# An unused 128 KB read of w_in put first on ScalarE's queue, in a kernel of chunked retention and a feed-forward block

## The chip, the core and the metric

The kernel runs on one core of a Trainium2 chip. The time is device microseconds (us) of one execution. The kernel before was timed in three runs: median 210.21 us, from 209.93 to 211.16 us. A profile was taken of one further execution.

The engines are named as in the profile: PE is TensorE (with PEld for its weight loads), DVE is VectorE, ACT is ScalarE, POOL is GpSimd and SP is SyncE. A transfer (DMA) is issued by one engine into that engine's queue, and its packets are then moved by the core's 16 DMA engines, which all queues share.

## The reference, cut to what matters

Two steps follow each other. The first is a recurrent retention layer: batch 4, 8 heads, 768 positions, head dimension 64, with one decay rate per head. The second is a feed-forward layer on the 3072 resulting rows, with a "snake" activation between its two matrix products.

```
gamma = 1.0 - 2.0 ** (-5.0 - np.arange(H))
for t in range(S):
    state = gamma * state + einsum('bhd,bhe->bhde', k[:, :, t], v[:, :, t])
    y[:, :, t] = scale * einsum('bhd,bhde->bhe', q[:, :, t], state)
x = y.transpose(0, 2, 1, 3).reshape(B * S, H * D)      # 3072 x 512
h = x @ w_in                                           # 3072 x 2048
s = np.sin(alpha * h)
g = h + s * s / (alpha + 1e-09)
out = g @ w_out                                        # 3072 x 512
```

Inputs and output are float32. The kernel computes its products in bf16.

## The kernel before, in words

**Tiling.** The recurrence is done in 24 chunks of 128 positions (6 per batch). A chunk is worked out with matrix products: scores inside the chunk, a decay mask, and for the later chunks of a batch a product with a running 64x64 state per head. The finished chunks, transposed, are collected in groups xT of 4, 2, 2, ..., 2, 4 chunks (`sizes`), and each group goes through the feed-forward: `Slot` does 128 columns of `x @ w_in` for a group (L496), the sine and the square on ACT (L499, L504) or DVE (L506), and the sum on DVE (L511); `ff_out` multiplies by w_out (L521); `take` and `last_tile` copy the sums out of PSUM and store them. The four first chunks of the batches, e0 to e3, need no state and come first.

**What sets the order.** The order of every engine's instructions is written out by hand, in program order (the pool's automatic scheduling is switched off by `manual_schedule`), and each engine works its list off in order. What ties the engines together is semaphores: an instruction waits for the data that it reads, and a transfer for the semaphore "lane" that an earlier transfer used (8 lanes for POOL's transfers, 8 for those of SP and ACT together, each used in turn).

**The start.** This is the part around the change.

- SP issues three transfers: q of chunk e0, then k of chunk e0 (L141, float32, 1024 pieces of 256 bytes each, tiles named `o_sb` because they borrow the buffers of the output), and alpha (L144).
- POOL issues all other loads, and they turn float32 into bf16 on the way: v of e0, then q, k, v of e1 and e2 (L100), the first quarter of w_in in two halves (L131), q and k of e3, the first quarter of w_out in two halves (L135), v of e3, the second quarters, and so on. Between them it computes small tables (L165 `tok`, L229 `qg`). From its ninth transfer on, one of POOL's transfers also waits until the one eight places earlier has landed.
- ACT loads the table for the exponential (L178), fills the decay table `dec` with eight activations (L190), turns k of e0 into bf16 (L576), and then copies results and fills `qg` (L569) until the first sine.
- DVE builds constants, turns q of e0 into bf16 (L574), and applies masks to scores (L286).
- PE fills its time with `idle_work`: matmuls on a zero tile, `spare<-warm` (L566), 25 in all, in counts written between the real steps. The first 9 stand ahead of the first real work, the transposes of q of e0 (L250). The real steps then are transposes (L250), scores (`stage_A`, L282), mixing with v (`stage_M`, L312), and from the group of e0 to e2 on the feed-forward.

ACT issues one transfer of its own in the kernel before, a 64 KB piece of the output at the very end (L553). Lines are those of the kernel before; behind the change the numbers are higher by 2.

Of the kernel before, what the change touches and what calls it, by code (L numbers as in the profile page):

```python
# [8 lines left out]
F32 = mybir.dt.float32  # L9
# [7 lines left out]
def kernel(  # L17
# [15 lines left out]
    nc = tc.nc  # L33
# [22 lines left out]
    consts = ctx.enter_context(tc.tile_pool(name="consts", bufs=1))  # L56
# [9 lines left out]
    w_in_v = moe_w_in.rearrange("(ko ki) f -> ki ko f", ki=128)  # L66
# [105 lines left out]
    load_w_out(1)  # L172


    warm = consts.tile([128, 512], BF16, name="warm")
    nc.vector.memset(warm, 0.0)  # L176
    tiny = consts.tile([128, 1], F32, name="tiny")
# [642 lines left out]
```

## Time and profile before

| what | value |
|---|---|
| time, median of 3 runs | 210.21 us (209.93 to 211.16) |
| the profiled execution's own time | 210.45 us |
| its span (first to last instruction) | 208.7 us |
| PE busy | 202.4 us, 97% of the span |
| DVE, ACT, POOL busy | 152.7, 151.6, 116.2 us |
| queue of POOL's transfers (software_dynamic) | 79248 packets, 13.38 MB |
| queue of SP's transfers (hardware_dynamic, q1) | 22608 packets, 10.96 MB |
| queue of ACT's one transfer (hardware_dynamic, q10) | 144 packets, 0.07 MB |
| read from and written to HBM | 27.27 MB and 6.29 MB |

How to read it: the span is what the profile covers, and the profiled execution's own time is 1.75 us longer. PE runs its list in order, so the end is the sum of its busy time and of the gaps in it; a gap counts when PE waits for something. The row DMA in the page's 40 slices shows how busy the 16 DMA engines were, in tenths. The list of transfers gives the time from issue to landing, which contains the wait behind earlier transfers.

### The profile page before, as it was taken

The page shows a single profiled execution, that of the slowest core. Times are in us where ns is not written, and L with a number is a line of the kernel's source. Part 1 is how long each engine was busy: PE and PEld are TensorE (multiplying, and loading weights), DVE is VectorE, ACT ScalarE, POOL GpSimd, SP SyncE. Part 2 cuts the span into 40 slices and gives each one's busy share as a digit, 9 for nine tenths or more (in the row PEclk, how much of TensorE's full clock was granted, in tenths as well). Part 3 has the DMA queues.
Part 4 walks back from the last instruction along what each step waited for, and adds up shares of the span by engine and source line. Part 5 has one row for each costly group of instructions (what it writes and reads, how often), then busy time and mean ns, then how long its engine had stood idle before and what let it go on. Part 6 is the DMA issues. An engine that isn't in the chain of part 4 may idle for free.

```text
span 208.7 us, 5765 instructions
## 1 busy us (share of the span) xinstructions
PE 202.4 (97%) x2370; PEld 123.7 (59%) x2370; DVE 152.7 (73%) x314; ACT 151.6 (73%) x309; POOL 116.2 (56%) x157
## 2 busy tenths in 40 slices
PE   7988999999999999999999999999999999999994
PEld 2444544467776766766666766666766664444453
DVE  5788688877989968768878868868888965656220
ACT  7777777657998787787687787686785779999001
POOL 8999847599999999999699910002022200000000
PEclk9999999999999999999999999999999999999999
DMA  9999999999999999999999996422412101010212
GB/s 132 148 167 194 202 201 185 154 168 196 162 115 154 104 187 171 170 110 194 171 117 169 152 143 53 104 60 44 105 56 48 53 2 50 2 50 3 101 50 101
DMA packets 102026, 24.76 MB, mean 119 GB/s; under 512 B 93024, under 2 KB 99056, under 8 KB 102000
## 3 DMA queue, kind: packets, MB, share of 16 engines
q0 software_dynamic: 79248, 13.38, 86.9%
q1 hardware_dynamic: 22608, 10.96, 24.0%
q8 instruction: 18, 0.29, 0.6%
q10 hardware_dynamic: 144, 0.07, 0.1%
q14 instruction: 8, 0.07, 0.1%
HBM read 27.27 MB, written 6.29 MB: 161 GB/s over the span
## 4 chain that ended last, share of the span: by engine, by line
PE 79%; DMA 9%; POOL 9%; issue 1%; DVE 0%; POOLq 0%; DVEq 0%
PE po L521 35%; PE ph L496 33%; DMA w_out<-in_moe_w_out_dram 5%; DMA qkr<-in_k_dram 5%; POOL qkr L100 3%; PE py L336 2%; POOL qg L229 2%; POOL vr L100 2%; PE poh L546 2%; POOL w_in L131 2%; PE py L390 1%; POOL w_out L135 1%; PE pa L346 1%; PE py L399 1%; PE pt L264 1%; PE pa L353 1%
## 5 line engine op out<-in xcount | busy, mean ns | idle before, releaser
L511 DVE SCALAR_TENSOR_TENSOR gT<-s,rec_alpha,ph 128x256 bf16<-128x256 f32 (+3 forms) x164 | 79.9, 523 | 31.7 <-ACT s L504 31.3
L496 PE MATMUL ph<-xT,w_in 128*128 128x256 bf16 (+3 forms) x656 | 98.6, 291 | 0.3 <-ACT xT L314 0.2
L499 ACT ACTIVATE s<-ph,alpha_sb 128x256 f32<-128x256 f32 (+3 forms) x164 | 76.1, 506 | 30.3 <-PE ph L496 30.2
L521 PE MATMUL po<-w_out,gT 128*128 128x512 bf16 x368 | 95.4, 380 | 0.0
L496 PEld LDWEIGHTS <-w_in 128*128 128x128 bf16 x656 | 63.3, 98 | 33.9 <-issue 1.2
L504 ACT ACTIVATE s<-s 128x512 f32<-128x512 f32 (+1 forms) x91 | 56.9, 625 | 2.9
L521 PEld LDWEIGHTS <-gT 128*128 128x128 bf16 x368 | 33.9, 98 | 29.6 <-DMA w_out<-in_moe_w_out_dram 0.2
L467 POOL CAST s_q<-s_f 128x256 bf16<-128x256 f32 x5 | 2.0, 396 | 35.6 <-DVE s_f L452 19.2
L533 DVE COPY o_sb<-po 128x512 f32<-128x512 f32 x20 | 13.8, 690 | 9.9 <-PE po L521 9.8
L120 POOL DMA_DIRECT2D qk_seq<-in_q_dram x24 | 16.9, 780 | 2.1 <-DMA v_seq<-in_v_dram 2.0
L120 POOL DMA_DIRECT2D qk_seq<-in_k_dram x24 | 16.9, 739 | 0.6 <-DMA qk_seq<-in_q_dram 0.5
L120 POOL DMA_DIRECT2D v_seq<-in_v_dram x24 | 16.9, 772 | 0.0
L156 POOL TENSOR_TENSOR v_seq<-v_seq,kgq 128x512 bf16<-128x512 bf16 x13 | 13.7, 1078 | 4.9 <-DMA v_seq<-in_v_dram 4.9
L441 DVE TENSOR_TENSOR xT<-py,qg 128x512 bf16<-128x512 f32 x19 | 13.0, 683 | 0.8 <-PE py L406 0.8
L361 DVE TENSOR_TENSOR aTw<-pa,maskq 128x768 bf16<-128x768 f32 x13 | 12.4, 951 | 0.0
L100 POOL DMA_DIRECT2D vr<-in_v_dram x11 | 10.2, 929 | 1.2 <-DMA w_in<-in_moe_w_in_dram 1.1
L566 PE MATMUL spare<-warm 128*128 128x512 bf16 x25 | 8.7, 471 | 1.2 <-DVE warm L176 1.2
L550 ACT COPY o_sb<-poh 128x256 f32<-128x256 f32 (+1 forms) x2 | 0.6, 319 | 11.7 <-PE poh L546 11.2
L349 DVE TENSOR_TENSOR aT<-pa,mask 128x1024 bf16<-128x1024 f32 x7 | 8.5, 1216 | 0.0
L467 ACT CAST s_q<-s_f 128x256 bf16<-128x256 f32 x14 | 5.5, 391 | 3.1 <-DVE s_f L461 2.7
L100 POOL DMA_DIRECT2D qkr<-in_k_dram x7 | 6.3, 899 | 1.7 <-DMA w_out<-in_moe_w_out_dram 1.7
L100 POOL DMA_DIRECT2D qkr<-in_q_dram x7 | 6.4, 910 | 1.0 <-DMA w_in<-in_moe_w_in_dram 1.0
(101 smaller groups left out, 162.3 us busy)
## 6 DMA issues: line engine op xcount, KB each, us to landing
out_dram<-o_sb SPq DMA_DIRECT2D x23, 256.0 KB, 3.0
w_in<-in_moe_w_in_dram POOLq DMA_DIRECT2D x6, 256.0 KB, 10.8
w_out<-in_moe_w_out_dram POOLq DMA_DIRECT2D x3, 512.0 KB, 11.0
vr<-in_v_dram POOLq DMA_DIRECT2D x11, 128.0 KB, 5.1
qk_seq<-in_q_dram POOLq DMA_DIRECT2D x16, 80.0 KB, 6.3
qk_seq<-in_k_dram POOLq DMA_DIRECT2D x16, 80.0 KB, 4.9
v_seq<-in_v_dram POOLq DMA_DIRECT2D x16, 80.0 KB, 5.6
qkr<-in_q_dram POOLq DMA_DIRECT2D x7, 128.0 KB, 5.7
```

Source lines behind the costliest of these rows:

```text
L100: nc.gpsimd.dma_start(out=t, in_=chunk_of(src, j))
L120: nc.gpsimd.dma_start(out=o, in_=src[bt, head(b, m, e), cs[0] * C:, :].rearrange("(f i) d -> i f d", i=64))
L156: eng.tensor_mul(t, t, by[:, j % NCH, :, None].to_broadcast([128, H, D]))
L361: return {"mask": lambda: nc.vector.tensor_mul(aT, pa[:, :, 0:384].rearrange("p e (m t) -> p e m t", m=2), maskq[:, None, None, :].to_broa ...
L441: nc.vector.tensor_mul(o, st["pyw", old][:, :, 0:256].rearrange("p b (m t) -> p b m t", m=2), by)
L496: nc.tensor.matmul(self.ph[:, m, :], w_in[:, i, f * 128:(f + 1) * 128], xT[g][:, i, self.lo:self.hi], start=(m == 0 and i == 0), stop=(i = ...
L499: nc.scalar.activation(out=self.s[:, m, :], in_=self.ph[:, m, :], func=ACTF.Sin, scale=alpha_sb[:, f:f + 1])
L504: nc.scalar.activation(out=self.s, in_=self.s, func=ACTF.Square)
L511: nc.vector.scalar_tensor_tensor(gT[self.g][:, f, self.lo:self.hi], self.s[:, m, :], rec_alpha[:, f:f + 1], self.ph[:, m, :], op0=ALU.mult ...
L521: nc.tensor.matmul(po[g, ts], gT[g][:, f, ts * C:(ts + 1) * C], w_out[:, f, :], start=(f == 0), stop=(f == FF - 1))
L533: nc.vector.tensor_copy(o_sb, po[g, ts])
L566: nc.tensor.matmul(spare["ps"], warm[:, :128], warm, start=True, stop=True)
```

## The change

Two lines are put ahead of ACT's first instruction. A new tile of 128 partitions by 256 float32 (1 KB in each partition) is allocated in the pool of constants, and ACT issues a transfer into it from the first 128 rows and first 256 columns of w_in, in float32, without a cast. Nothing reads the tile. The same numbers are still loaded by POOL as before.

```diff
     load_w_in(1)
     load_w_out(1)
 
+    wake = consts.tile([128, 256], F32, name="wake")
+    nc.scalar.dma_start(out=wake, in_=w_in_v[:, 0, 0:256])
     warm = consts.tile([128, 512], BF16, name="warm")
     nc.vector.memset(warm, 0.0)
     tiny = consts.tile([128, 1], F32, name="tiny")
```

The order of instructions on every engine is otherwise the same: ACT has one more, the transfer, ahead of its first table load, and PE, DVE, POOL and SP have the same lists. Since the lanes of SP's and ACT's transfers are used in turn, each later one of these has the next lane (q of e0 now signals on the second lane instead of the first, and so on), with the same distance of eight. The tiles allocated after `wake` lie 1 KB further on in each partition.

## The prediction

> **What bounds the kernel now.** I read the page first, for the engines and the chain.
>
> ```profile
> PE 202.4 (97%) x2370; PEld 123.7 (59%) x2370; DVE 152.7 (73%) x314; ACT 151.6 (73%) x309; POOL 116.2 (56%) x157
> ...
> PE   7988999999999999999999999999999999999994
> ...
> DMA  9999999999999999999999996422412101010212
> ...
> q0 software_dynamic: 79248, 13.38, 86.9%
> ```
>
> PE is busy for 202.4 of 208.7 us, with a fixed list of instructions, so all gaps of PE together are 6.3 us. The DMA row is full from the first slice to the twenty-fourth (about 125 us): a transfer added in that time can only displace others. Next, the timeline of the first 21 us (start, duration, engine, line, what, count, idle before), for the place of the change.
>
> ```profile
> 0.74 1.28 ACT L178 ACT_TABLE_LOAD   x1 [0.74 <-PEq L804]
> 0.74 0.46 SPq L141 DMA_DIRECT2D o_sb<-in_q_dram  x1
> ...
> 1.19 4.02 PE L566 MATMUL spare<-warm 128*128 128x512 bf16 x9 [1.19 <-DVE warm L176]
> ...
> 2.52 2.45 ACT L190 ACTIVATE dec<-tio,back 128x128 f32<-128x128 f32 x8 [0.28 <-DVE mask L192]
> ...
> 3.92 0.55 DVE L574 CAST qb<-o_sb 128x512 bf16<-128x512 f32 x1 [0.42 <-DMA o_sb<-in_q_dram]
> ...
> 4.58 0.15 PEld L250 LDWEIGHTS <-qb 128*128 128x128 bf16 x1 [0.28 <-DVE qb L574]
> 5.00 0.61 PE L250 MATMUL pt<-ident,qb 128*128 128x128 bf16 x4
> ...
> 5.17 0.62 ACT L576 CAST kb<-o_sb 128x512 bf16<-128x512 f32 x1 [0.21 <-DMA o_sb<-in_k_dram]
> ...
> 20.42 0.41 PE L312 MATMUL pye<-aT,vr 128*64 128x128 bf16 x8 [0.66 <-DMA vr<-in_v_dram]
> ```
>
> PE has fillers until about 5.0 us, while q of e0 is ready at 4.47 (3.92 + 0.55): q has some 0.42 us in hand (weights at 4.58, matmul at 5.00). k of e0 has none: ACT stands idle 0.21 us for it. Later, at 20.42, PE stands 0.66 us for v of e3, whatever happened before. Last, the chain in order of time up to 41 us (start, duration, what).
>
> ```profile
> 16.76 3.98 POOL qg L229 x4
> 20.74 9.94 DMA w_out<-in_moe_w_out_dram
> 30.68 0.28 issue
> 30.96 9.53 DMA qkr<-in_k_dram
> ...
> 40.54 0.41 PE pt L264 x8
> ```
>
> The chain runs through POOL's transfers until 40.54 us and through PE alone after that. So what a few hundred ns in the start are worth is decided by one question: do POOL's transfers land later? PE has idle time of 0.26 us between 40 and 60 us and almost none from 60 to 160, so a shift at 40.54 reaches the end whole.
>
> **The change, part by part.**
>
> *Nothing is removed.* No wait on the data of the new tile exists. The lanes of SP's and ACT's later transfers move by one with the same distance of eight, and the unused read has landed tens of us before its lane comes up again. I cost that at nothing.
>
> *ACT's instruction.* One issue ahead of the table load. Rows: SP's first issue takes 0.46 us, ACT's own issue at the end 0.37, SP's second 0.56. ACT starts at 0.74, so the table load ends 0.37 to 0.56 later, at 2.39 to 2.58 instead of 2.02, and `tiny` (0.20) at 2.59 to 2.78. `dec` started at 2.52 after 0.28 idle on DVE's mask, so it moves by 0.07 to 0.26 and ends at 5.04 to 5.23. The next on ACT is k at 5.17, which waits for its transfer anyway: ACT costs at most 0.06 us, taken as 0. The cover is the idle 0.28 and 0.21; without it all 0.37 to 0.56 would go to k. DVE reads `dec` first at 5.99, so it does not notice.
>
> *The packets, on SP's two loads.* 128 packets of 1 KB, 131 KB. The nearest row is the first half quarter of w_in on POOL's queue, which reads the same kind of 1 KB pieces (and writes 512 bytes): from 11 to 13 us 708 packets went through in 2 us, 354 per us. 128 of them take 0.36 us of all 16 engines. The other bound is SP's rate for 256 byte pieces, about 280 GB/s around 3 us: 131 KB / 280 = 0.47 us. From below, the read can fall into time when the DMA engines have nothing to do: the first packets of q start 1.1 us after their issue and ACT's last transfer starts its packets 0.88 us after its own, so the read can be up to 0.26 us ahead of q; then 0.1 us is left, and if it is quicker still, 0. I take 0.36, since the two issues start at the same 0.74 us and both find an idle chip. q then is ready at 4.83, inside its 0.42 of cover: nothing. k lands at 5.53 instead of 5.17 and PE's transposes of it, with all that follows on PE, ACT and DVE, move by 0.36. This lasts until 20.42, where the 0.66 us of waiting for v of e3 swallows it. What counts from there is how late v of e3 comes.
>
> A rule of the Trainium skill, "DMA: Bandwidth & Descriptors", section "Issuing engines are not separate DMA queues", says that transfers issued by different engines run on the same 16 DMA engines and interleave; by it the read delays q, k and POOL's loads alike. By the ceiling of 435 GB/s of the same page ("Where 436 GB/s comes from") the 131 KB would take an estimated 0.30 us, which is 0.06 us less than the row's 0.36 and would lower the sum below by as much.
>
> *The packets, on POOL's loads.* The engines are busy from about 2 us on, so 0.36 us of work is pushed ahead of POOL's first load. Can they catch up? From 5 to 9.5 us POOL's queue moved 5296 packets, 1177 per us, and every load landed 4.5 to 4.7 us after its issue: no backlog builds up, POOL's issuing (0.87 us for 1024 packets, 1177 per us) sets the pace. From 37.5 to 41 us, behind a backlog, the same kind of packet went at 4291 in 3.5 us, 1226 per us. So the DMA engines have 49 of 1226, 4%, to spare, over some 5 us (4.6 to 9.6): 0.20 us is caught up. After that w_in comes in, the time to landing grows (7.6 us for v of e3, issued at 12.81) and nothing more can be caught up until 40 us. So v of e3 and all later loads come 0.36 - 0.20 = 0.16 us later. Bounds: 0 (the read fits in idle time or is caught up) and 0.47 (none caught up). POOL's issues wait for landed transfers and move by the same 0.16.
>
> *Sum.* PE at 20.42 moves by 0.16, at 40.54 by 0.16 (its loads come by as much later), and the rest of the list follows. The profiled execution took 210.45 us (span 208.7 plus 1.75 around it) and would become 210.6; it lies 0.24 above the median of the three runs, 210.21. On the median the forecast is 210.4 us, with its own range from 210.2 (nothing) to 210.7 (0.47). The three runs before reach from 209.93 to 211.16, so the draw itself adds about 0.3 below and 0.5 above.
>
> **The rivals.**
>
> *It gains: the read wakes something.* SP's first packets came 1.1 us after the issue; SP's outputs late in the kernel, on idle DMA engines, come 0.83 after theirs. If a first transfer pays 0.3 us for being first, and ACT's read pays in q's place, q and k come up to 0.3 us earlier. For: this difference. Against: both are issued at 0.74 us, so both pay at once; and k's gain ends at 20.42, where PE waits for a load of POOL's, issued at 12.81 after a chain of POOL alone. Time: 210.2, and if POOL's loads gained the whole 0.3 as well, 209.9. Over 1% is hardly to be had at all: of PE's 6.3 us of gaps 1.2 lie ahead of the first filler and about 3 behind the last matmul, which leaves 2.1 us, the 1% itself.
>
> *It loses much: PE's clock.* The nine first fillers take 4.02 us, 0.45 each; the five at 11.90 us take 1.25, 0.25 each, though the page shows a full granted clock throughout. PE runs at about half speed until some time after 5 us. If q comes after the fillers end, that is later by more than its 0.42 us, PE gets a gap just before the change of speed, and the speed may come a stretch later. Price: one more stretch as long as the first, some 3 to 4 us with about 3 us of PE work at half speed, +3 us, less the 0.66 swallowed at 20.42: 212.6. For: 0.47, my upper bound, is just past 0.42, and an issue by ACT could hold up SP's (0.37 more), if the two share what makes the descriptors. Against: by 0.36 the cover holds, and a gap of 0.1 us in 4 is little. The Trainium skill ("TensorE: Matmul & The Clock Gate", "Part 1: The HAM clock gate") has the clock rise after a busy window of about 3.4 us that runs freely; by it such a gap would matter only if it fell into the deciding window. The trace agrees as to the size: 4 us at half speed.
>
> *SP is held up, without the clock.* If SP's two issues stand behind ACT's 0.37 us, k comes 0.36 + 0.37 = 0.73 later, 0.07 more than the 0.66 at 20.42 swallow, less than POOL's 0.16: no change of the sum, 210.4.
>
> *Nothing at all.* The read falls wholly into the idle time ahead of q's first packet: 210.2.
>
> **How the numbers follow.** Slower by 0 to 0.5 us as worked out (SP held up is part of it): 0.60. Nothing at all, within 0.1 us: 0.13. A small gain: 0.07. The clock, or another lasting loss of over 2 us that I do not see: 0.14. A gain over 2 us by a way that the traces do not show: 0.06. About 1% (2.1 us) is what a measurement of this kernel can tell from no change. So: faster by over 1% 0.06, within 1% 0.80, slower by over 1% 0.14. The time is that of the likeliest, 210.4. The range takes in the small gain and the draw of the runs below (209.7) and above the bound of 210.7 with the draw (211.2); it leaves out the two far cases.
>
> **What would show it.** Right: ACT's first instruction a transfer of about 0.4 us, its table load ending near 2.4; `qb` at 4.2 to 4.3 and `kb` at about 5.5 instead of 3.92 and 5.17; PE's wait at `pye` L312 shorter than 0.66, and that instruction at 20.5 to 20.6; the transposes behind `qkr` at about 40.7; the rest shifted whole. Wrong: `kb` at 5.17 or earlier (the read was free, or it wakes); `pye` at 20.42 or earlier; fillers at 0.4 us after 6 us (the clock); a gap in PE after 60 us that was not there, or a loss that arises where POOL's loads did not come later.

## The result, and the profile after

The changed kernel takes 211.10 us (median of 18 runs, 210.93 to 211.51), the kernel before 210.22 us beside it (18 runs, 209.88 to 211.20). The ratio is 1.0038, 95% interval 1.0026 to 1.0049: slower by 0.5 to 1.0 us, inside the 1% that was called no change, but some four times the forecast +0.19 us and above the forecast's own range (210.7). Two experiments below (`e5_late`, `e8_double`) had their profiles taken in disturbed executions, so their times are used and, of the profile of `e5_late`, only the place of its issue.

The start of the changed kernel, from its timeline (start, duration, engine, line, what, count, idle before):

```profile
0.74 0.43 ACTq L176 DMA_DIRECT2D wake<-in_moe_w_in_dram  x1
0.74 0.46 SPq L141 DMA_DIRECT2D o_sb<-in_q_dram  x1
...
1.19 4.02 PE L568 MATMUL spare<-warm 128*128 128x512 bf16 x9 [1.19 <-DVE warm L178]
...
1.20 1.28 ACT L180 ACT_TABLE_LOAD   x1 [1.20 <-PEq L806]
...
2.60 2.43 ACT L192 ACTIVATE dec<-tio,back 128x128 f32<-128x128 f32 x8
...
5.21 0.43 DVE L576 CAST qb<-o_sb 128x512 bf16<-128x512 f32 x1 [1.70 <-DMA o_sb<-in_q_dram]
...
5.69 0.61 PE L252 MATMUL pt<-ident,qb 128*128 128x128 bf16 x4 [0.47 <-DVE qb L576]
...
6.48 0.62 ACT L578 CAST kb<-o_sb 128x512 bf16<-128x512 f32 x1 [1.45 <-DMA o_sb<-in_k_dram]
...
20.71 0.42 PE L314 MATMUL pye<-aT,vr 128*64 128x128 bf16 x8
```

ACT's part is as forecast: 0.43 us of issue, `dec` over at 5.03, in time. But q is cast at 5.21 instead of 3.92 and k at 6.48 instead of 5.17, 1.3 us later each, not 0.36. PE's fillers end near 5.2 us and it then stands for q. At `pye`, the mixing of e3, the wait for v of e3 is gone from PE's row: something else now comes last there.

Why q is late is in the transfers. Queues at work from 1.8 to 2.4 us and from 2.4 to 3.4 us (packets, MB, share of 16 engines), first of the kernel before:

```profile
q1 hardware_dynamic: 308, 0.08, 56.6%
...
q1 hardware_dynamic: 1061, 0.27, 118.3%
```

and of the changed kernel:

```profile
q10 hardware_dynamic: 61, 0.06, 59.9%
...
q10 hardware_dynamic: 80, 0.07, 39.2%
q1 hardware_dynamic: 322, 0.08, 36.0%
```

Queue 10 is ACT's, queue 1 SP's. In the first 0.6 us not one packet of q moves, although both were issued at 0.74, and the read crawls: 61 packets in 0.6 us is 100 per us, against 354 per us for pieces that read 1 KB in the saturated stream, on POOL's queue, that the forecast took. The list of transfers gives the outcome (median us from issue to landing; before, 3.2, 3.9 and 4.8 for q, k and POOL's first v):

```profile
o_sb<-in_q_dram SPq DMA_DIRECT2D x1, 256.0 KB, 4.4
wake<-in_moe_w_in_dram ACTq DMA_DIRECT2D x1, 128.0 KB, 3.3
...
o_sb<-in_k_dram SPq DMA_DIRECT2D x1, 256.0 KB, 5.2
vr<-in_v_dram POOLq DMA_DIRECT2D x1, 128.0 KB, 6.0
```

POOL's loads start late by the same 1.2 us and catch up, but not before w_in comes in: v of e3, issued at 12.96 instead of 12.81, lands after 7.4 instead of 7.6 us, while k of e2, issued at 6.10 instead of 5.92, lands at 11.91 instead of 10.61. PE's transposes of q and k of e2 show it, first in the kernel before:

```profile
9.74 0.40 PE L250 MATMUL pt<-ident,qkr 128*128 128x128 bf16 x4
...
10.65 0.40 PE L250 MATMUL pt<-ident,qkr 128*128 128x128 bf16 x4
```

and in the changed kernel, with some pieces of its chain (start, duration, what):

```profile
11.06 0.40 PE L252 MATMUL pt<-ident,qkr 128*128 128x128 bf16 x4 [0.37 <-DMA qkr<-in_q_dram]
...
6.10 5.81 DMA qkr<-in_k_dram
...
11.95 0.41 PE pt L252 x4
...
13.31 1.22 DVE aT L288
...
19.53 1.13 DVE aT L288
```

The chain leads from POOL's load of k of e2 through PE, ACT and DVE to the masked scores (`aT`) that `pye` reads. They are ready at 20.66, in the kernel before at 19.58. PE stands 0.37 us for q of e2 at 11.06, so in this profile the late q and k of e0 had that much in hand: the loss at `pye` came by POOL's loads.

The span grew by 0.5 us in this pair of profiles (the medians lie 0.9 apart, and the pair does not show the rest), in two steps. From 20.42 to 20.71 at `pye` it is 0.3. The rest comes at 57 us, where PE waits in the changed kernel's timeline for the first transfer that transposes:

```profile
49.24 10.31 SPq L275 DMA_TRANSPOSE qkT<-qkr  x3
...
57.19 0.42 PE L348 MATMUL pa<-qkT 64*64 64x128 bf16 x16 [0.20 <-DMA qkT<-qkr]
```

It was issued earlier than before (49.24, before 50.00) but took 7.9 us to land, before 5.0.

### The profile page after: what moved, and what is told of

It reads as the page before. It is cut to its first block, busy times and chain, and to the rows that moved or that the text cites. A ratio compares the mean times of both kernels' runs of the same rounds, so it can differ in the third digit from the quotient of the medians.

```text
span 209.2 us, 5740 instructions
## 1 busy us (share of the span) xinstructions
PE 199.6 (95%) x2343; PEld 123.7 (59%) x2370; DVE 152.3 (73%) x314; ACT 151.6 (72%) x309; POOL 116.4 (56%) x157
## 4 chain that ended last, share of the span: by engine, by line
PE 83%; DMA 7%; DVE 3%; POOL 2%; issue 2%; ACT 2%; POOLq 0%; DVEq 0%; ACTq 0%
PE ph L498 37%; PE po L523 35%; DMA qkT<-qkr 4%; DMA qkr<-in_k_dram 3%; PE py L338 2%; PE poh L548 2%; PE py L392 1%; POOL qkr L100 1%; DVE aT L288 1%; POOL vr L100 1%; DVE gT L513 1%; ACT s L501 1%; PE pt L266 1%; ACT s L506 1%; PE pa L348 1%
## 5 line engine op out<-in xcount | busy, mean ns | idle before, releaser
L523 PE MATMUL po<-w_out,gT 128*128 128x512 bf16 x346 | 91.3, 380 | 3.2 <-issue 2.7
L156 POOL TENSOR_TENSOR vr<-vr,kg 128x512 bf16<-128x512 bf16 x5 | 5.5, 1103 | 3.4 <-DMA vr<-in_v_dram 3.4
```

The lines of the kernel that those rows point to most:

```text
L156: eng.tensor_mul(t, t, by[:, j % NCH, :, None].to_broadcast([128, H, D]))
L523: nc.tensor.matmul(po[g, ts], gT[g][:, f, ts * C:(ts + 1) * C], w_out[:, f, :], start=(f == 0), stop=(f == FF - 1))
```

## The experiments

Theory S: the read holds up q and k of e0, and POOL's loads, in the first microseconds, and what of that is left at `pye` is the loss. Theory T, in later expectations, adds that at `pye` only what exceeds the landing of v of e3 counts. Each kernel below is the changed kernel with one edit, unless it says otherwise.

**Is it the bytes at all?** `e3_small` reads only 16 pieces of 256 bytes:

```diff
-    nc.scalar.dma_start(out=wake, in_=w_in_v[:, 0, 0:256])
+    nc.scalar.dma_start(out=wake[0:16, 0:64], in_=w_in_v[0:16, 0, 0:64])
```

> ACT's first transfer is cut to 16 pieces of 256 bytes (4 KB); its issue on ACT, the 1 KB tile and the lanes moved by one stay. Theory S (the loss comes from the 128 KB holding up q and k of e0): q is cast at 3.9 to 4.1 us and k at 5.2 to 5.4, and the time is that of before within 0.15 us. Rival L (the loss comes from ACT's extra issue, the moved lanes or the moved tiles): 0.5 to 0.9 us slower, as with the full read.

Measured: q 4.14, k 5.43, ratio to before 0.9989 (0.9978 to 1.0000). Both casts come a little later than expected, but so they do in `b1_v_earlier` below (4.17 and 5.44), which has no read at all: that much is the difference between executions. ACT's issue, the moved lanes and the moved tiles cost nothing; rival L falls.

**Does it matter who is in front?** `e4_sp` issues the same read from SP, behind q, k and alpha:

```diff
-    nc.scalar.dma_start(out=wake, in_=w_in_v[:, 0, 0:256])
+    nc.sync.dma_start(out=wake, in_=w_in_v[:, 0, 0:256])
```

> The same 128 KB, issued by SP behind alpha and not by ACT, so that q and k are ahead of it in one queue. Theory S: q at 3.92 and k at 5.17 as before; POOL's first loads a little later; the time that of before to 0.2 us more. Rival P (the bytes push POOL's loads back, whoever issues them): the loss of 0.5 to 0.9 us stays, with POOL's loads landing later from 6 us on.

Measured: q 4.11, k 5.36, ratio 1.0010 (0.9997 to 1.0022). The loss is mostly gone. Its profile still shows POOL's loads later, and PE waits for them with q and k of e0 almost in time (PE's waits from 8 to 60 us: total, times, longest):

```profile
PE pt L252 <- DMA qkr<-in_q_dram: 0.5, 1, 0.5
...
PE pt L252 <- DMA qkr<-in_k_dram: 0.3, 1, 0.3
```

k of e2 lands at 11.43, 0.8 us later than before and not 1.3. v of e3 lands 7.9 us after the issue at 12.81, and PE waits 0.46 us for it at 20.77, 0.35 later than in the profile of before. So rival P has a share, up to 0.5 us. The run does not part q and k of e0 from POOL's loads, since both come earlier here than in the changed kernel.

`e5_late` moves ACT's issue behind its table load in the program. Its profile has the issue at 1.17 us, while the table load still runs, and not at the 2.0 that was expected.

> The same 128 KB issued by ACT, but behind its table load and the first small activation, at about 2.0 us, when q's and k's descriptors are on their way. Theory S with the queues served in turn: q at 3.9 to 4.1, k at 5.3 to 5.9, loss 0 to 0.4 us. If ACT's queue is served ahead of SP's whenever it has packets: k at 6.0 or later, loss 0.3 to 0.9 us.

Measured: ratio 0.9999 (0.9986 to 1.0011). Issued 0.43 us later, the same 128 KB cost nothing that shows.

**Why is the read slow?** `e1_contig` reads one contiguous block, `e6_pitch2k` pieces 2 KB apart (of w_out), `e2_pieces` 512 pieces of 256 bytes 8 KB apart, `e7_half` half as many pieces:

```diff
-    nc.scalar.dma_start(out=wake, in_=w_in_v[:, 0, 0:256])
+    nc.scalar.dma_start(out=wake, in_=moe_w_in[0:16, :].rearrange("a (b c) -> (a b) c", c=256))   # e1_contig
+    nc.scalar.dma_start(out=wake, in_=moe_w_out[0:128, 0:256])                                     # e6_pitch2k
+    nc.scalar.dma_start(out=wake.rearrange("i (a c) -> i a c", a=4), in_=w_in_v[:, :, 0:64])       # e2_pieces
+    nc.scalar.dma_start(out=wake[0:64], in_=w_in_v[0:64, 0, 0:256])                                # e7_half
```

> ACT first reads the same 128 pieces of 1 KB into the same tile, but from the first 16 whole rows of w_in, so one contiguous block instead of pieces 8 KB apart. Theory A (the read was slow, 1.5 us instead of 0.36, because its pieces lie 8 KB apart): the packets are through in about 0.4 us, q is cast at about 4.3 and k at 5.5, and the loss shrinks to 0.1 to 0.3 us. Rival B (large packets on DMA engines that have just started are slow wherever they lie): q at about 5.2, k at about 6.5, loss 0.5 to 0.9 us.

> ACT first reads 128 pieces of 1 KB that lie 2 KB apart (the first half of 128 rows of w_out) and not 8 KB apart. If the distance makes the read slow, this lies between the contiguous block (k at 5.78) and the 8 KB (k at 6.48): k at 5.8 to 6.2, loss 0.1 to 0.4 us. If only the contiguous block is quick: k at 6.4 to 6.6 and a loss of 0.7 to 0.9 us.

> ACT first reads the same 128 KB of w_in, but as 512 pieces of 256 bytes, the first 256 bytes of all 512 rows, all 8 KB apart. If the size of the pieces made the read slow: it runs at the 1100 pieces per us of q, is through in 0.5 us, q at 4.4 to 4.6, k at 5.7 to 5.9, loss 0 to 0.2 us. If the distance of 8 KB made it slow (all pieces fall on few memory channels): no faster than before, q at 5.2 or later, k at 6.5 or later, loss 0.7 us or more.

> ACT first reads half as much, 64 pieces of 1 KB at 8 KB distance. k lands about half as late, at 5.7 to 5.9. Theory T: `pye` still waits for v of e3, and the time is that of before to 0.2 us more. Rival (the loss is in proportion to the lateness of k, whatever waits later): 0.4 to 0.5 us slower.

Measured (casts, landings and `pye` in one profile each; the second row of the changed kernel is `a1_again`, below):

| kernel | read lands after | q | k | k of e2 lands | v of e3 lands | `pye` starts, its wait for v of e3 | span | ratio to before |
|---|---|---|---|---|---|---|---|---|
| before | | 3.92 | 5.17 | 10.61 | 20.38 | 20.42, 0.66 | 208.7 | 1 |
| e3_small | 1.6 | 4.14 | 5.43 | 10.84 | 19.63 | 19.88, none | 208.1 | 0.9989 |
| e4_sp | 3.9 | 4.11 | 5.36 | 11.43 | 20.72 | 20.77, 0.46 | 208.9 | 1.0010 |
| e1_contig | 2.6 | 4.50 | 5.78 | 11.20 | 20.09 | 20.14, 0.07 | 208.5 | 1.0003 (0.9987 to 1.0020) |
| e6_pitch2k | 2.9 | 4.83 | 6.10 | 11.53 | 20.60 | 20.65, 0.24 | 208.8 | 1.0003 (0.9986 to 1.0020) |
| e2_pieces | not listed | 5.16 | 6.48 | 11.91 | 20.63 | 20.72, none | 209.0 | 1.0015 (0.9992 to 1.0039) |
| e7_half | 4.5 | 5.46 | 6.58 | 11.88 | 20.98 | 21.03, 0.28 | 209.2 | 1.0013 (0.9992 to 1.0034) |
| changed | 3.3 | 5.21 | 6.48 | 11.91 | 20.38 | 20.71, none | 209.2 | 1.0038 (1.0026 to 1.0049) |
| changed, again | 3.4 | 5.40 | 6.66 | 12.09 | 21.07 | 21.48, none | 209.7 | 1.0044 (1.0027 to 1.0061) |

Two of POOL's loads rule the column of `pye`. In the six rows from `e4_sp` to the first of the changed kernel, `aT` is ready 8.75 to 8.76 us after k of e2 lands, whether k of e0 is cast at 5.36 or at 6.58, and `pye` starts then or at the landing of v of e3, whichever is later. In the other three `aT` comes 8.97 to 9.34 us after k of e2, so something else ended last: in the second profile of the changed kernel PE's slow clock (below), and in `e3_small` too the chain leads back through PE's fillers.

The distance of the pieces goes with the lateness, with one profile for each: 1, 2 and 8 KB apart, the read lands after 2.6, 2.9 and 3.3 us and k is cast at 5.78, 6.10 and 6.48. The queues of `e1_contig` in the two stretches shown above:

```profile
q10 hardware_dynamic: 63, 0.06, 83.3%
...
q1 hardware_dynamic: 854, 0.22, 96.0%
q10 hardware_dynamic: 80, 0.07, 19.3%
```

The first 0.6 us are as slow as with 8 KB (63 packets; with 2 KB it is 93); what the contiguous block gains comes after 2.4 us, where q gets 854 packets through and not 322. Smaller pieces did not help, and half the bytes came no earlier: both expectations of size fail, and lateness here is not in proportion to bytes. In both of these kernels SP's queue went first (247 packets in `e2_pieces` and 310 in `e7_half` from 1.8 to 2.4 us, none of ACT's), and q still landed 4.4 and 4.7 us after its issue. So standing behind the read does not explain the late q by itself. Why half as many pieces landed last of all, 4.5 us after the issue, is open.

**Is the step at 57 us part of the change?**

> The changed kernel, unaltered, for a second profile. Theory T (a threshold: PE's own chain from k of e0 reaches the mixing of e3, `pye`, 4.9 us after its first feed-forward matmul, and only what exceeds the landing of v of e3 counts): k at 6.3 to 6.6, `pye` at 20.6 to 20.8 with no wait for v of e3, 0.7 to 0.9 us slower. Of that, the second step of +0.3 to +0.4 us at 57 us, behind the first transfer that transposes, is either seen again (then it belongs to the change) or not (then it was an accident of one execution, and the loss up to 42 us must be larger than the 0.3 of the first profile).

Measured: no wait for a transposing transfer in this profile, nor in those of the other kernels of the table and of `e9_fill`: the step belongs to that one execution, as far as these profiles show. Instead this profile has another addition. Its start, from the timeline:

```profile
6.28 0.61 PE L252 MATMUL pt<-ident,qb 128*128 128x128 bf16 x4 [1.07 <-DVE qb L576]
...
6.68 1.06 PE L568 MATMUL spare<-warm 128*128 128x512 bf16 x2
...
7.96 1.06 PE L568 MATMUL spare<-warm 128*128 128x512 bf16 x2
...
21.48 0.41 PE L314 MATMUL pye<-aT,vr 128*64 128x128 bf16 x8
```

PE's gap is 1.07 us here, and its fillers still take 1.06 us for two at 7.96, where the first profile of the changed kernel has this:

```profile
6.09 1.06 PE L568 MATMUL spare<-warm 128*128 128x512 bf16 x2
...
7.39 0.59 PE L568 MATMUL spare<-warm 128*128 128x512 bf16 x2
```

The trace's record of the granted clock has full speed from 10.04 us, against 7.11 in the first profile and 5.46 in that of before (the expectation below has the first two 0.24 us too late). `pye` is 0.77 later with k only 0.18 later. v of e3 landed at 21.07, and by the landings alone `pye` would start at an estimated 21.1, so the slow clock cost about 0.4 us there. That is the clock rival of the prediction.

Whether the gap made the clock late is not shown by this. The gap is longer mostly because DVE's cast of q took 0.82 us here and 0.43 in the first profile. And with no gap ahead of it full clock came anywhere from 3.94 us (`e1_contig`) to 6.75 us (`e3_small`); only the 10.04 lies far outside.

`e9_fill` gives PE two more fillers ahead of q:

```diff
-    idle_work(9)
+    idle_work(11)
```

> The changed kernel with 11 instead of 9 fillers ahead of the transposes of q, so that PE has work until about 6 us and no gap while q is late. If the late rise of PE's clock (10.28 us in the second profile of the changed kernel, 7.35 in the first) comes from the gap of 0.5 to 1.1 us: the rise is at 4 to 7.7 us, the changed kernel's upper group of runs (211.4 to 211.5) is gone, and the median is 210.6 to 211.0, no slower than the changed kernel although PE has two matmuls more. Rival (the clock's rise is chance, the gap has no part in it): the upper group stays, and the median is 211.1 to 211.6. Either way q stays at about 5.2 and k at about 6.5. A first transposing transfer that lands near 57 us with PE waiting for it, as in the first profile of the changed kernel, would leave the median at 211.0; without it, 210.7.

Measured: ratio 1.0027 (1.0014 to 1.0039), 211.11 us, 210.86 to 211.26 in 12 runs; full clock from 4.33 us, while the first nine fillers still ran, so this profile says nothing of the two that were added. The group above 211.3, 10 of the 28 runs of the changed kernel, is gone, as the gap theory has it. The median is not better: PE ran its 11 fillers faster, had a gap of 1.01 us all the same, and in this profile v of e3 came last:

```profile
21.30 0.41 PE L314 MATMUL pye<-aT,vr 128*64 128x128 bf16 x8 [0.32 <-DMA vr<-in_v_dram]
```

**More of it.** `e8_double` reads 256 pieces (`w_in_v[:, 0:2, 0:256]` into a tile of 2 KB per partition).

> ACT first reads twice as much, 256 pieces of 1 KB at 8 KB distance. Theory T: past the threshold each us that k is later costs about 0.8 us; k at 7.4 to 8.0, `pye` at 21.4 to 22.0 with no wait for v of e3, 1.6 to 2.2 us slower than before. Rival (the loss is a fixed price, as of a missed step of the clock or of one late transposing transfer): 0.6 to 1.0 us slower, as with 128 KB.

Measured: 211.47 us, the median of only three runs, ratio 1.0060 (1.0042 to 1.0078), 0.9 to 1.6 us slower. It grows with the read, by less than expected; the interval still touches the fixed price of 0.6 to 1.0.

**A better version?** Both are the kernel before with v of e3 issued between the halves of w_out; the second has k of e0 issued by ACT too:

```diff
-    for h in range(2):
-        load_w_out(0, h)
-    load_chunk(order[3], "v")
+    load_w_out(0, 0)
+    load_chunk(order[3], "v")
+    load_w_out(0, 1)
...
-        nc.sync.dma_start(out=near[name], in_=chunk_of(src, 0))
+        (nc.sync if name == "q" else nc.scalar).dma_start(out=near[name], in_=chunk_of(src, 0))   # b2_v_k
```

> The kernel before, without the read, and POOL's load of v of e3 issued between the two halves of the first quarter of w_out instead of behind them. Theory T (before, v of e3 ends PE's wait at `pye`, and its landing varies): v of e3 lands about 1 us earlier, `pye` at 19.6 to 19.8 without a wait, 0.3 to 0.6 us faster than before, and the runs lie closer together than before. If loads at 40 us set the end anyway: no change, 0 to 0.1 us.

> As the last, and k of e0 is issued by ACT as its first instruction, so that it goes out at 0.74 us and not at 1.26 behind q. Theory T, with q and k served in turn: q later (4.3 to 4.8), k at about 5.0 or earlier, PE's chain 0 to 0.3 us earlier than in the last kernel, 0.3 to 0.8 us faster than before. If ACT's queue goes ahead of SP's on each DMA engine, as the packets of the changed kernel suggest: k at 4.1 to 4.4 and q at 4.9 to 5.2, so that q becomes the late one, and the time lies 0 to 0.4 us above the last kernel's.

Measured: 1.0003 (0.9993 to 1.0014) and 1.0002 (0.9987 to 1.0016). In the profiles `pye` starts at 19.73 and 19.63 without a wait and the spans are 208.1 and 208.0 us, but the medians are no faster: this part of theory T fails. The runs of the first lie somewhat closer (209.87 to 210.65 in 12, before 209.80 to 211.18 in 23), those of the second do not (209.77 to 211.00). With q and k on two queues, q is cast at 4.65 and k at 5.43: here SP's queue went first, with 262 packets from 1.8 to 2.4 us and none of ACT's.

## Why the prediction was right and wrong

**What held.** The direction. Nothing from the lanes, the tiles and ACT's issue (`e3_small`). That the bytes in front of others are the price. That it comes down to whether POOL's loads land later: in the six rows of the table from `e4_sp` to the first of the changed kernel, `pye` starts by k of e2 or by v of e3. That `pye` is the place where it is decided: in the ten profiles of the table and of `e9_fill`, span less start of `pye` is 188.1 to 188.5 us.

**The first term that was mis-sized: the packets on SP's two loads.** 0.36 us became 1.3 (1.0 against `b1_v_earlier`, which has no read either). The row taken was a stream that had run for some time at 354 pieces per us; the first pieces went at 100 per us. My upper bound, 0.47, rested on a running stream as well. In the changed kernel's profiles q's packets came behind the read's (queues from 1.8 to 2.4 us), in `e2_pieces`, `e7_half` and `b2_v_k` SP's came first, so the order of queues is not fixed. The Trainium skill's rule that queues share the same engines ("DMA: Bandwidth & Descriptors", "Issuing engines are not separate DMA queues") was borne out by the landings: q, k and POOL's v of e0 all land 1.2 to 1.3 us later. The estimate of 0.30 us from that page's ceiling, as my 0.36, was far too low.

**The second, and the step that failed with it: the packets on POOL's loads.** The forecast was 0.36 - 0.20 = 0.16 us, with the 0.20 caught up from 4.6 to 9.6 us and nothing after that until 40. It was the other way round. From v of e0 to k of e2 POOL's loads land 1.2 to 1.3 us later, with nothing caught up; w_in then lands 0.3 later, and v of e3 at 20.38 as before. Since the forecast looked at v of e3 alone, it put PE's own waits for the loads of e2 at nothing. By that way the 0.66 us of cover at `pye`, rightly read, was too small: `aT` came 1.08 us later (20.66 for 19.58), and `pye` 0.29.

v of e3 itself landed between 20.1 (`e1_contig`) and 21.25 us (`e9_fill`) in kernels with the full read in front, 20.4 in the profile of before, 19.6 in `e3_small`. One profile each does not say how much of this is the read and how much the execution.

**At 40.54 us** a shift of 0.08 was seen (40.62 in the changed kernel), where 0.16 was forecast: PE's transposes start later there by 0.39 (40.37 for 39.98) and no longer wait in their midst for `qkr`. The 0.3 us crossed that point on DVE, whose mask of the scores starts at 40.99 instead of 40.60, and was back on PE at 42.26 (before 41.99).

**The clock rival** shared its 0.14 with other losses of over 2 us and was priced at 212.6. It happens, but smaller: as far as two profiles tell, in the third or so of the runs above 211.3, at some 0.4 us.

**Luck.** 211.10 lies inside the wide range, up to 211.2, only because 0.5 us had been added there for the draw of the runs. It covered two terms that were too small.

**Open:** why the first pieces go so slowly; the bulk of the changed kernel's runs (210.93 to 211.16) lies 0.25 us above those of `e2_pieces` (210.69 to 210.96 but for one), with the same k, the same k of e2 and the same `pye` in the profiles; and what makes runs of before spread over 1.3 us.

## What to carry to other kernels

Price a transfer that stands first by the first transfers of the trace and not by a saturated stream: here 1 KB pieces went at 100 per us at the start and at 354 per us in the stream. What else is issued at that moment comes later, in whichever queue it is; issued a little later (`e4_sp`, `e5_late`) the same bytes cost between nothing and 0.5 us. Follow every load that the delay pushes back to the first instruction that needs it, and not only the one that is waited for today: here the path moved to another load. And a wait that "swallows" a delay has a size: compare it with the largest delay that you cannot exclude, not with the likeliest.

## What the runs showed of the hardware

Full clock on PE came at 3.94 to 6.75 us in profiles with no gap ahead of it, at 7.11 behind a gap of 0.47 us and at 10.04 behind one of 1.07 us; `e9_fill`, with a gap of 1.01 us but the clock already up at 4.33, did not lose it. For 128 pieces of 1 KB read first of all, the landing came 2.6, 2.9 and 3.3 us after the issue with 1, 2 and 8 KB between them in memory (one profile each, the second of another tensor). And two transfers issued at the same 0.74 us on SP's and ACT's queues were not always served in the same order: from 1.8 to 2.4 us only ACT's packets moved in the changed kernel, only SP's in `e2_pieces`, `e7_half` and `b2_v_k`.
